# Score maxima from four 32x32 array tiles, score stacks kept per head in DRAM, and a lagged inverse DFT step

## The chip, the cores and the metric

The kernel runs on one core of one Trainium2 chip. The metric is the time of one execution on the device in microseconds (us); lower is better. Before the change three runs took 1411.7, 1414.9 and 1418.0 us, median 1414.9 us. A core has a matrix engine (TensorE, rows PE and PEld), a vector engine (VectorE, DVE), a scalar engine (ScalarE, ACT), GpSimd (POOL) and SyncE (SP), whose queue issues nearly all DMA transfers here. Each takes its instructions in order; they wait for each other through semaphores.

## The reference, cut to what matters

Two branches that share nothing are computed and put side by side in the output:

```python
def _A_ref(x, wqkv, wo):                      # x [1,2048,576], sliding-window attention
    B, S, D = x.shape
    H = 32; Dh = D // H; W = 256
    qkv = (x @ wqkv).reshape(B, S, 3, H, Dh).transpose(2, 0, 3, 1, 4)
    q, k, v = qkv[0], qkv[1], qkv[2]
    scores = einsum("bhqd,bhkd->bhqk", q, k) * (Dh ** -0.5)
    mask = (idx[:, None] - idx[None, :] >= 0) & (idx[:, None] - idx[None, :] < W)
    p = softmax(where(mask, scores, -1e9))
    o = einsum("bhqk,bhkd->bhqd", p, v)
    return o.transpose(0, 2, 1, 3).reshape(B, S, D) @ wo

def _B_ref(u, A, B, C, log_dt, Dskip):        # u [1,2048,576], S4 convolution
    K = real(sum_n C * dt*B * exp(dt*A*l))    # 2048 taps of each of 576 channels
    y = irfft(rfft(pad(u)) * rfft(pad(K)))[:2048]
    return y + u * Dskip

out = concatenate([_A_ref(...), _B_ref(...)], axis=-1)
```

32 heads of 18 channels; a query sees the 256 keys up to its own position.

## The kernel before

**Stage one (0 to 475 us)** interleaves three generators: `proj` (Q, K and V in f16 hi/lo pairs; Q and K written to DRAM as `qd`, V as `vd`), `tables` (the taps of the convolution) and `s1_u` (first DFT step of u, written to `gx`). `s1_k` does the same for the taps (`gk`). In `qd` there are three planes of 1152 rows: for a query row hi, lo, hi, for a key row hi, hi, lo. 54 rows, three planes of a head's 18 channels, stand under one another in a *stack*, so that one product gives hi·hi + lo·hi + hi·lo.

**The attention stage (from about 537 us)** is written out by hand: `attention` runs over 16 units, half `hf` of the queries by group `g` of four heads, and cuts a unit into six items (`c`, `bank`). For each item `merge` interleaves `scores` of the item (score matmuls L640 into PSUM `ST`, the exponential on ACT L642, masks on POOL L651), seven of the 32 steps of `gmax` of the *next* unit, `values` of the item two back (L663 into `po`), and two or three steps of `conv`. Python order is the order of each engine's queue. The sixth item of a unit has no `gmax` step left.

- `gmax` finds each query's maximum over its window. For 32 queries of four heads a block-diagonal tile `qh` (96 rows by 128 columns, loaded with the other heads' places zero) is the stationary operand: one matmul (L602) gives the scores of 128 rows by 288 keys, a second (L605, or L608 at the sequence's start) adds the mask from `bias`, and DVE takes the maximum (L610). The 128x32 maxima are turned (L614) and written by four small DMAs (L619) into row 54 of `Q`, against a key row of -32768: so the next unit's scores come out with the maximum subtracted. The PSUM pool `ring`, three banks, is shared by `gmax`, `conv` and the output projection.
- `load_unit(i + 1)` (eight stack loads L587 and L588, V by L591) and `load_gmax(i + 2)` (four loads into `qh` in pieces of 64 bytes, L575, one of `kh`, L577) are issued on SP at the start of unit i. Both exist in two sets.
- `norm` divides by the softmax's sum: `den` gathers the sum rows by a DMA (L678), reciprocal on DVE (L680), to DRAM `rd` (L682), back as `rb` on all 128 partitions (L684), the multiplication on DVE (L687), a hi/lo pair (L689, L690), and four DMAs to `od` (L693). It goes on by one `yield` per item.
- `conv` does 16 pairs of frequencies by two halves `hs`: four products (L477) with u's and the taps' first step, complex multiplication on DVE (t, L493 to L498; Y, L502 and L503), and the inverse (L507), whose result an ACT or DVE copy puts into `ho`, then DRAM `h`. After all pairs, 16 rounds `qd` read `h` back (L518) and u (L522), multiply u by the skip weight on POOL (L530), do the last inverse (L534), add on DVE (L536) and store (L539).
- `wo(0)` runs the output projection of the first half from item 62, `wo(1)` that of the second after everything else.

Of the kernel before, what the change touches and what calls it, by code (L numbers as in the profile page):

```python
# [97 lines left out]
def conv_steps(n):  # L98

    return (n + 1) * 225 // 96 - n * 225 // 96  # L100


class Kernel:
# [50 lines left out]

    def proj(self):
        nc, a, wp, dp, sp = self.nc, self.a, self.p["wq"], self.p["dram"], self.p["const"]
        self.qd = dp.tile([3, 1152, L], F16, name="qd")
# [33 lines left out]
        for c in range(4):  # L191
# [13 lines left out]
            for m in range(9):  # L205
                ps = self.p["pps"].tile([128, 512], F32, name="pp")
                self.mm14(ps, (wh, wl), (xh, xl), slice(m * 128, m * 128 + 128), slice(0, 512))
                st = self.p["pst"].tile([128, 2, 512], F16, name="qst")
                nc.scalar.activation(st[:, 0], ps, AF.Copy, scale=S)  # L209
                nc.vector.scalar_tensor_tensor(st[:, 1], ps, S, st[:, 0], op0=OP.mult, op1=OP.subtract)  # L210
                for r0, r1, two, one in ((0, D, slice(0, 2), 2), (D, 2 * D, slice(0, 3, 2), 1)):
                    r0, r1 = max(r0, m * 128), min(r1, m * 128 + 128)
                    if r0 < r1:
                        v = st[r0 - m * 128:r1 - m * 128]
                        nc.sync.dma_start(self.qd[two, r0:r1, cs].rearrange("a p c -> p a c"), v)
                        nc.sync.dma_start(self.qd[one, r0:r1, cs], v[:, 0])
                yield
# [239 lines left out]
    def conv(self):  # L457
# [22 lines left out]

        nx = load(0)
        for fp in range(16):
            cu, nx = nx, load(fp + 1) if fp < 15 else None
            ho = fs.tile([128, 2, D], F32, name="ho")
            for hs in range(2):
                X = fy.tile([128, 2, 288], F32, name="X")
                t1 = fy.tile([128, 2, 288], F32, name="t1")
                t2 = fy.tile([128, 2, 288], F32, name="t2")
                for p in range(2):
                    self.evac(X[:, p], s2(cu["w2"], cu["tx"], p, hs))  # L490
                    yield
                kr = s2(cu["w2"], cu["tk"], 0, hs)
                tt(t1[:, 0], X[:, 0], kr, op=OP.mult)  # L493
                tt(t2[:, 1], X[:, 1], kr, op=OP.mult)
                yield
                ki = s2(cu["w2"], cu["tk"], 1, hs)
                tt(t2[:, 0], X[:, 1], ki, op=OP.mult)
                tt(t1[:, 1], X[:, 0], ki, op=OP.mult)  # L498
                Y = [fy.tile([128, 288], F32, name="Y%d" % par) for par in range(2)]
                for par in range(2):  # L500
                    sl = slice(64 * par, 64 * par + 64)
                    tt(Y[par][0:64], t1[sl, 0], t2[sl, 0], op=OP.subtract)  # L502
                    tt(Y[par][64:128], t1[sl, 1], t2[sl, 1], op=OP.add)  # L503
                yield
                for par in range(2):
                    ps = ring()
                    nc.tensor.matmul(ps, cu["i1"][:, par, :], Y[par], start=True, stop=True)  # L507
                    self.evac(ho[:, par, hs * 288:hs * 288 + 288], ps)
                    yield
            nc.sync.dma_start(self.h.rearrange("a l f d -> (a l) f d")[:, 2 * fp:2 * fp + 2, :], ho)  # L510
# [3 lines left out]
        def loadh(qd):  # L514
            hp = fs.tile([128, 2, D], F32, name="ho")
# [4 lines left out]
            ut = fs.tile([128, D], F32, name="tx")  # L520
            for k in range(4):
                nc.sync.dma_start(ut[32 * k:32 * k + 32], uw[4 * qd + k])  # L522
# [19 lines left out]
    def att_setup(self):  # L542
# [10 lines left out]
        for b in range(2):  # L553
            d = {"q": ap.tile([96, 32, 4, 32], F16, name="qh%d" % b), "k": ap.tile([96, HK], F16, name="kh%d" % b),
                 "Q": ap.tile([128, 2, HQ], F16, name="Q%d" % b), "K": ap.tile([128, 2, HK], F16, name="K%d" % b)}
            nc.gpsimd.memset(d["q"], 0.0)
            nc.vector.memset(d["k"][64:96], 0.0)
# [12 lines left out]
    def load_gmax(self, i):  # L570

        nc, (hf, g), d = self.nc, divmod(i, 8), self.sets[i % 2]
        q0, k0, kc, kn = self.cols(hf)
        for j in range(4):
            nc.sync.dma_start(d["q"][18 * j:18 * j + 18, :, j, :],  # L575
                              self.qd[0, 72 * g + 18 * j:72 * g + 18 * j + 18, q0:q0 + HQ].rearrange("p (s q) -> p s q", q=32))
        nc.sync.dma_start(d["k"][0:72, kc:kc + kn], self.qd[0, D + 72 * g:D + 72 * g + 72, k0:k0 + kn])  # L577

    def load_unit(self, i):

        nc, (hf, g), d = self.nc, divmod(i, 8), self.sets[i % 2]
        q0, k0, kc, kn = self.cols(hf)
        t0, tn = k0 // 128, kn // 128
        for u in range(2):
            for b in range(2):
# [4 lines left out]
        nc.vector.memset(V[:, 760:], 0.0)  # L590
        nc.sync.dma_start(V[:, 760 - 76 * tn:760].rearrange("p (t e) -> p t e", e=76), self.vd[g][:, t0:t0 + tn])  # L591
        self.V[i] = V

    def gmax(self, i):
        nc, (hf, g), d = self.nc, divmod(i, 8), self.sets[i % 2]
        m = self.p["m"].tile([128, 32], F32, name="m")
        for t in range(32):
# [4 lines left out]
            nc.tensor.matmul(ps[:, :n], d["q"][:, t].rearrange("p j q -> p (j q)"), d["k"][:, k0:k0 + n],  # L602
                             start=True, stop=False, skip_group_check=True)
# [69 lines left out]
    def norm(self, i):  # L673
# [4 lines left out]
        nc.sync.dma_start(den, osb[18:128:32])  # L678
# [5 lines left out]
        nc.sync.dma_start(rb, rd.unsqueeze(1).to_broadcast([4, 32, HQ]))  # L684
# [4 lines left out]
        nc.scalar.activation(h[:, 0], osb, AF.Copy)  # L689
        nc.vector.tensor_tensor(h[:, 1], osb, h[:, 0], op=OP.subtract)  # L690
        for j in range(4):
            f0 = 72 * g + 18 * j
            nc.sync.dma_start(self.od[:, f0:f0 + 18, HQ * hf:HQ * hf + HQ].rearrange("a p n -> p a n"),  # L693
                              h[32 * j:32 * j + 18])
        yield

# [96 lines left out]
    def build(self):  # L793
        nc, a = self.nc, self.a
        with ExitStack() as es:
# [29 lines left out]
            with ExitStack() as e1:  # L825
# [5 lines left out]
                for n, b, s in (("fs", 2, None), ("fy", 2, None), ("att", 1, None), ("m", 2, None), ("P", 4, None),  # L831
                                ("v", 3, None), ("o", 2, None), ("n", 2, None), ("wo", 1, None), ("wo2", 2, None),
# [37 lines left out]
```

## Time and profile before

The profiled execution took 1412.87 us, its span 1411.2 us; the granted TensorE clock was 0.828 of full speed on average.

| engine | busy us | share of the span |
|---|---|---|
| PE, matmuls | 974.2 | 69% |
| PEld, weight loads | 473.1 | 34% |
| DVE | 713.4 | 51% |
| ACT | 610.4 | 43% |
| POOL | 338.6 | 24% |

167.06 MB went over the DMA queues, 161.30 MB of it issued by SP. Busy PE time holds matmuls from issue to modelled end, so that one which waits in the array counts as busy. A wait is named by who ended it. The attention stage is read by its units: the boundaries used here are the issue times of the V load (L591), which comes once in a unit.

### The profile page before, as it was taken

The page shows a single profiled execution, that of the slowest core. Times are in us where ns is not written, and L with a number is a line of the kernel's source. Part 1 is how long each engine was busy: PE and PEld are TensorE (multiplying, and loading weights), DVE is VectorE, ACT ScalarE, POOL GpSimd, SP SyncE. Part 2 cuts the span into 40 slices and gives each one's busy share as a digit, 9 for nine tenths or more (in the row PEclk, how much of TensorE's full clock was granted, in tenths as well). Part 3 has the DMA queues.
Part 4 walks back from the last instruction along what each step waited for, and adds up shares of the span by engine and source line. Part 5 has one row for each costly group of instructions (what it writes and reads, how often), then busy time and mean ns, then how long its engine had stood idle before and what let it go on. Part 6 is the DMA issues. An engine that isn't in the chain of part 4 may idle for free.

```text
span 1411.2 us, 25678 instructions
## 1 busy us (share of the span) xinstructions
PE 974.2 (69%) x10314; PEld 473.1 (34%) x10314; DVE 713.4 (51%) x1369; ACT 610.4 (43%) x907; POOL 338.6 (24%) x340
## 2 busy tenths in 40 slices
PE   1538898898889873777756686687678667645537
PEld 0224464464555431232212232233234333111115
DVE  3797667677662441555625565466445435322110
ACT  2767687687762311343423343344333324212212
POOL 0024344353440100222211122122112112323310
PEclk9759999999999985878857688899889889766769
DMA  9553143233224664234334424345335333556632
GB/s 240 156 175 115 59 114 87 81 83 103 70 55 135 185 181 124 68 118 112 115 85 114 133 63 136 110 126 144 87 105 150 76 120 87 137 153 168 170 94 101
DMA packets 199112, 167.06 MB, mean 118 GB/s; under 512 B 72945, under 2 KB 171057, under 8 KB 198801
## 3 DMA queue, kind: packets, MB, share of 16 engines
q1 hardware_dynamic: 197440, 161.30, 40.3%
q10 hardware_dynamic: 1504, 3.99, 1.1%
q8 instruction: 81, 1.33, 0.4%
q14 instruction: 39, 0.31, 0.1%
q0 software_dynamic: 48, 0.13, 0.0%
HBM read 103.11 MB, written 61.87 MB: 117 GB/s over the span
## 4 chain that ended last, share of the span: by engine, by line
PE 35%; DMA 21%; DVE 18%; SPq 12%; ACT 7%; issue 6%; POOL 1%; DVEq 0%; ACTq 0%; POOLq 0%
PE pp L153 7%; SPq L575 6%; PE po L663 4%; PE r L477 4%; PE r L153 4%; PE r L602 3%; DMA Q<-qd 3%; PE kp L395 3%; PE ST L640 3%; DMA rb<-rd 3%; PE pp L438 2%; PE r L507 2%; DMA den<-osb 2%; DVE m L610 2%; DMA oh<-od 2%
## 5 line engine op out<-in xcount | busy, mean ns | idle before, releaser
L642 ACT ACTIVATE P<-ST,esc 128x1024 f32<-128x1024 f32 (+1 forms) x192 | 202.9, 1060 | 291.9 <-PE ST L640 285.4
L651 POOL TENSOR_SCALAR_AFFINE_SELECT P<-P 128x512 f32<-128x512 f32 x240 | 156.3, 681 | 597.1 <-ACT P L642 597.0
L610 DVE TENSOR_REDUCE m<-r 128x1 f32<-128x288 f32 (+7 forms) x512 | 198.2, 430 | 167.5 <-PE r L605 117.6
L602 PE MATMUL r<-kh,qh 96*128 96x288 f16 (+7 forms) x512 | 144.2, 316 | 94.6 <-DVE m L610 59.3
L357 POOL TENSOR_TENSOR m<-A,tr 128x1024 f32<-128x1024 f32 x72 | 149.8, 2103 | 192.5 <-PE kp L395 145.8
L663 PE MATMUL po<-P,V 128*32 128x256 f32 (+2 forms) x1408 | 133.7, 458 | 4.5 <-ACT osb L671 2.1
L395 PE MATMUL kp<-Q,m 128*32 128x64 f32 x4608 | 87.0, 229 | 28.1 <-DVE Q L378 10.7
L640 PE MATMUL ST<-Q,K 64*128 64x384 f16 (+2 forms) x704 | 85.3, 313 | 22.3 <-DMA Q<-m 14.5
L602 PEld LDWEIGHTS <-qh 96*128 96x128 f16 x512 | 54.7, 108 | 115.9 <-issue 78.2
L395 PEld LDWEIGHTS kp<-Q,m 128*32 128x32 f32 x4608 | 74.3, 115 | 55.5 <-issue 41.1
L605 PE MATMUL r<-bias,idb 128*128 128x64 bf16 x448 | 91.2, 210 | 0.0
L507 PE MATMUL r<-Y,i 128*128 128x288 f32 x128 | 63.5, 587 | 35.6 <-DVE Y L503 13.2
L438 PE MATMUL pp<-ut,w 128*128 128x288 f32 x128 | 51.3, 525 | 45.0 <-DMA ut<-in_u_dram 27.5
L605 PEld LDWEIGHTS <-idb 128*128 128x128 bf16 x448 | 46.6, 104 | 91.8 <-issue 86.0
L534 PE MATMUL r<-ho,i 128*64 128x288 f32 x128 | 31.4, 580 | 62.7 <-DMA ho<-h 60.4
L477 PE MATMUL r<-tx,w 128*64 128x288 f32 x256 | 53.1, 499 | 30.2 <-DMA tx<-gx 22.5
L536 DVE TENSOR_TENSOR tk<-r,tx 128x288 f32<-128x288 f32 x32 | 14.3, 455 | 100.7 <-POOL tx L530 87.8
L153 PE MATMUL r<-woh,oh 128*128 128x288 f16 x160 | 29.5, 320 | 49.5 <-DMA oh<-od 49.4
L788 ACT ACTIVATE ya<-r,osc 128x288 f32<-128x288 f32 x32 | 16.0, 501 | 102.8 <-PE r L153 83.7
L210 DVE SCALAR_TENSOR_TENSOR qst<-pp,qst 128x512 f16<-128x512 f32 x36 | 24.7, 686 | 64.1 <-ACT qst L209 64.1
L153 PEld LDWEIGHTS <-oh 128*128 128x128 f16 x320 | 33.1, 107 | 68.1 <-DMA oh<-od 51.0
L116 ACT ACTIVATE g<-pp 128x288 f32<-128x288 f32 (+1 forms) x84 | 34.6, 447 | 45.7 <-DMA gk<-g 21.8
(150 smaller groups left out, 1667.2 us busy)
## 6 DMA issues: line engine op xcount, KB each, us to landing
gx<-g SPq DMA_DIRECT2D x32, 288.0 KB
gk<-g SPq DMA_DIRECT2D x16, 576.0 KB
tx<-gx SPq DMA_DIRECT2D x16, 576.0 KB
tk<-gk SPq DMA_DIRECT2D x16, 576.0 KB
h<-ho SPq DMA_DIRECT2D x16, 576.0 KB
ho<-h SPq DMA_DIRECT2D x64, 144.0 KB
raw<-in_xT_dram SPq DMA_DIRECT2D x16, 512.0 KB
qd<-qst SPq DMA_DIRECT2D x32, 256.0 KB
```

What stands on the lines that cost most here:

```text
L153: self.nc.tensor.matmul(ps, u, v, start=(i == 0), stop=(i == len(ops) - 1))
L357: self.nc.gpsimd.tensor_tensor(m, A[:, ch, a0:a0 + 8].unsqueeze(3).to_broadcast(sh), tr[:, ch, part, 0:8].unsqueeze(2).to_broadcast(sh), o ...
L395: nc.tensor.matmul(kp[32 * st:32 * st + 32, c % 2 * JJ2 + j, :], m[:, ch, a0:a0 + 32], Q[:, ch, term % 2, :], start=(term == 0), stop=(ter ...
L477: nc.tensor.matmul(ps[64 * par:64 * par + 64], w2[:, par, 64 * part:64 * part + 64], t[:, 2 * hs:2 * hs + 2, par, :], start=True, stop=True)
L507: nc.tensor.matmul(ps, cu["i1"][:, par, :], Y[par], start=True, stop=True)
L602: nc.tensor.matmul(ps[:, :n], d["q"][:, t].rearrange("p j q -> p (j q)"), d["k"][:, k0:k0 + n], start=True, stop=False, skip_group_check=True)
L605: nc.tensor.matmul(ps[:, :288].rearrange("p (a b) -> p a b", b=32)[:, 0:9:8], self.idb, self.bias, start=False, stop=True, skip_group_chec ...
L610: nc.vector.tensor_reduce(m[:, t:t + 1], ps[:, :n], axis=AX.X, op=OP.max)
L640: nc.tensor.matmul(ps[:, u, o:o + n], d["K"][h, jp, k0:k0 + 128], d["Q"][h, jp, q0:q0 + n], start=True, stop=True, skip_group_check=True)
L642: nc.scalar.activation(pt[:, 2 * jp:2 * jp + 2, lo:hi], ps[:, :, lo:hi], AF.Exp, scale=self.esc)
L651: nc.gpsimd.affine_select(v, v, pattern=[[0, 4], [sg, 128]], compare_op=OP.is_ge, fill=0.0, base=-1 if far else 0, channel_multiplier=-sg)
L663: nc.tensor.matmul(self.po[32 * j:32 * j + 32, t0 * 128:t1 * 128], V[:, kb * 76 + 19 * j:kb * 76 + 19 * j + 32], pt[:, j, o:o + (t1 - t0) ...
```

## The change

- `proj`: the Q and K columns of `wqkv` are put in another order on the host, channel by channel with the 64 heads of a channel side by side, so that a projection tile of 128 rows holds two channels of all heads. `store_heads` writes 54 rows of a head as one block of `qd`: hi, hi, lo for queries and hi, lo, hi for keys. Six DMAs per tile replace two (four in one tile).
- `gmax` uses the stacks `Q` and `K` of `scores`: their first 32 rows, which hold 18 hi·hi and 14 of the 18 cross products. Four matmuls per step, each on an array tile of 32 rows by 32 columns, replace the one. `qh`, `kh` and `load_gmax` go.
- Three sets of `Q` and `K` instead of two; `load_unit(i + 2)` at the start of unit i, four stack loads instead of eight. V loads, `od` stores and u loads are issued by POOL instead of SP.
- `norm`: `den` and `rb` in four DMAs each, one more item between `den` and its reciprocal and one between the hi and lo halves.
- `conv`: Y on POOL instead of DVE; the inverse of a half step is issued after the next half's Y; its copies and X's are all on ACT; the next pair is loaded in the middle of a pair; `h` rounds are loaded two ahead, after six empty steps. 232 steps are spread over the 96 items instead of 225.

```diff
 def conv_steps(n):
-    return (n + 1) * 225 // 96 - n * 225 // 96
+    return (n + 1) * 232 // 96 - n * 232 // 96
...
+    def store_heads(self, st, i, cs):
+        nc = self.nc
+        stack = lambda o, n: self.qd[18 * o:18 * o + 54 * n, cs].rearrange("(h a r) c -> h a r c", a=3, r=18)[:, :, i]
+        nc.sync.dma_start(stack(1, 64)[:, 0:2], st)
+        nc.sync.dma_start(stack(0, 32)[:, 0], st[0:32, 0])
+        nc.sync.dma_start(stack(97, 32)[:, 2], st[32:64, 0])
...
-                        nc.sync.dma_start(self.qd[two, r0:r1, cs].rearrange("a p c -> p a c"), v)
-                        nc.sync.dma_start(self.qd[one, r0:r1, cs], v[:, 0])
+                for e in range(2):
+                    self.store_heads(st[64 * e:64 * e + 64], 2 * m + e, cs)
...
+        def inverse(fp, hs, i1, Y, ho):
+            for par in range(2):
+                ps = ring()
+                nc.tensor.matmul(ps, i1[:, par, :], Y[par], start=True, stop=True)
+                nc.scalar.activation(ho[:, par, hs * 288:hs * 288 + 288], ps, AF.Copy)
+                yield
+            if hs == 1:
+                nc.sync.dma_start(self.h.rearrange("a l f d -> (a l) f d")[:, 2 * fp:2 * fp + 2, :], ho)
...
-                    tt(Y[par][0:64], t1[sl, 0], t2[sl, 0], op=OP.subtract)
-                    tt(Y[par][64:128], t1[sl, 1], t2[sl, 1], op=OP.add)
+                    nc.gpsimd.tensor_tensor(Y[par][0:64], t1[sl, 0], t2[sl, 0], op=OP.subtract)
+                    nc.gpsimd.tensor_tensor(Y[par][64:128], t1[sl, 1], t2[sl, 1], op=OP.add)
                 yield
+                if last:
+                    yield from inverse(*last)
+                last = fp, hs, cu["i1"], Y, ho
+                if hs == 0 and fp < 15:
+                    nx = load(fp + 1)
...
-                nc.sync.dma_start(ut[32 * k:32 * k + 32], uw[4 * qd + k])
+                nc.gpsimd.dma_start(ut[32 * k:32 * k + 32], uw[4 * qd + k])
...
-        nx = loadh(0)
-        yield
+        nx = [loadh(0), loadh(1)]
+        for _ in range(6):
+            yield
...
         for u in range(2):
-            for b in range(2):
-                r = 72 * g + 36 * b + 18 * u
-                nc.sync.dma_start(d["Q"][64 * u:64 * u + 54, b], self.qd[:, r:r + 18, q0:q0 + HQ])
-                nc.sync.dma_start(d["K"][64 * u:64 * u + 54, b, kc:kc + kn], self.qd[:, D + r:D + r + 18, k0:k0 + kn])
+            nc.sync.dma_start(d["Q"][64 * u:64 * u + 54], heads(216 * g, q0, HQ)[u])
+            nc.sync.dma_start(d["K"][64 * u:64 * u + 54, :, kc:kc + kn], heads(32 * 54 + 18 + 216 * g, k0, kn)[u])
...
-            nc.tensor.matmul(ps[:, :n], d["q"][:, t].rearrange("p j q -> p (j q)"), d["k"][:, k0:k0 + n],
-                             start=True, stop=False, skip_group_check=True)
+            for j in range(4):
+                r = slice(64 * (j % 2), 64 * (j % 2) + 32)
+                nc.tensor.matmul(ps[32 * j:32 * j + 32, :n], d["Q"][r, j // 2, 32 * t:32 * t + 32],
+                                 d["K"][r, j // 2, k0:k0 + n], start=True, stop=False, skip_group_check=True)
...
-        nc.sync.dma_start(den, osb[18:128:32])
+        for j in range(4):
+            nc.sync.dma_start(den[32 * j:32 * j + 32], osb[32 * j + 18:32 * j + 19])
+        yield
         yield
...
-        nc.sync.dma_start(rb, rd.unsqueeze(1).to_broadcast([4, 32, HQ]))
+        for j in range(4):
+            nc.sync.dma_start(rb[32 * j:32 * j + 32], rd[j].partition_broadcast(32))
...
-                    self.load_unit(i + 1)
                     if i < 14:
-                        self.load_gmax(i + 2)
+                        self.load_unit(i + 2)
...
-                                ("v", 3, None), ("o", 2, None), ("n", 2, None), ("wo", 1, None), ("wo2", 2, None),
+                                ("v", 4, None), ("o", 3, None), ("n", 2, None), ("wo", 1, None), ("wo2", 2, None),
```

The order of instructions on PE, in the second unit (i = 1), at one `gmax` step behind `values` (`po`) and an inverse of `conv` (`r<-Y`). Before:

```order
L663 MATMUL po<-P,V 32x128 x4
L507 MATMUL r<-Y_6555,i_6161 128x288
L602 LDWEIGHTS qh_5942
L602 MATMUL r<-kh_5943,qh_5942 128x288
L605 LDWEIGHTS idb
L605 MATMUL r<-bias,idb 128x2x32
```

After the change, at such a place:

```order
L670 MATMUL po<-P,V 32x256 x4
L488 MATMUL r<-Y_6798,i_6533 128x288
L609 LDWEIGHTS Q_6092
L609 MATMUL r<-K_6093,Q_6092 32x288
L609 LDWEIGHTS Q_6092
L609 MATMUL r<-K_6093,Q_6092 32x288
L609 LDWEIGHTS Q_6092
L609 MATMUL r<-K_6093,Q_6092 32x288
L609 LDWEIGHTS Q_6092
L609 MATMUL r<-K_6093,Q_6092 32x288
L612 LDWEIGHTS idb
L612 MATMUL r<-bias,idb 128x2x32
```

One pair of weight load and matmul on the whole array has become four pairs on tiles of 32x32, and the mask's matmul on the whole array still follows each group of four.

SP at the start of a unit, from the stack loads to the softmax sum of the unit before. Before:

```order
L587 DMA Q_5955<-qd 54x1x1024
L588 DMA K_5956<-qd 54x1x1024
L591 DMA V<-vd 128x608
L575 DMA qh_5942<-qd 18x32x32 x4
L577 DMA kh_5943<-qd 72x1024
L678 DMA den<-osb 128x1x32
L682 DMA rd<-den 128x32
L684 DMA rb<-rd 128x1x1024
```

After:

```order
L591 DMA Q_6078<-qd 54x2x1024
L592 DMA K_6079<-qd 54x2x1024
L591 DMA Q_6078<-qd 54x2x1024
L592 DMA K_6079<-qd 54x2x1024
L492 DMA h<-ho 128x1152
L469 DMA w_6905<-in_c_w_dram 128x256
L469 DMA i_6907<-in_c_i_dram 128x256
L472 DMA tx<-gx 128x4x288
L472 DMA tk<-gk 128x4x288
L686 DMA den<-osb 32x1x32 x4
L691 DMA rd<-den 128x32
L694 DMA rb<-rd 32x1024 x4
```

The five `gmax` loads and V are gone from ahead of `den`, and the loads of `conv` stand in their place.

POOL within a unit, after the change (before, it held nothing but L651 rows there, 136 in a row):

```order
L595 DMA V<-vd 128x608
L516 TENSOR_TENSOR Y_7793<-t_7709,t_7710 64x288
L517 TENSOR_TENSOR Y_7793<-t_7709,t_7710 64x288
L516 TENSOR_TENSOR Y_7794<-t_7709,t_7710 64x288
L517 TENSOR_TENSOR Y_7794<-t_7709,t_7710 64x288
L658 AFFINE_SELECT P<-P 128x4x128 x2
L704 DMA od<-oh_7762 18x2x1024 x4
L658 AFFINE_SELECT P<-P 128x4x128
L516 TENSOR_TENSOR Y_8003<-t_7894,t_7895 64x288
```

Y and three kinds of DMA have come in between the masks (L658), which wait for nobody but ACT's exponential.

More of the change, by code (lines that the diff above doesn't have):

```diff
@@ L210, in proj @@
                 nc.vector.scalar_tensor_tensor(st[:, 1], ps, S, st[:, 0], op0=OP.mult, op1=OP.subtract)
[L211 to L216, printed above, removed]
+                for e in range(2):
+                    self.store_heads(st[64 * e:64 * e + 64], 2 * m + e, cs)
                 yield
@@ L479, in s2 @@
             return ps
+        def inverse(fp, hs, i1, Y, ho):
[6 more added lines that the diff above has]
+                nc.sync.dma_start(self.h.rearrange("a l f d -> (a l) f d")[:, 2 * fp:2 * fp + 2, :], ho)
         nx = load(0)
+        last = None
         for fp in range(16):
-            cu, nx = nx, load(fp + 1) if fp < 15 else None
+            cu = nx
             ho = fs.tile([128, 2, D], F32, name="ho")
@@ L501, in conv @@
                     sl = slice(64 * par, 64 * par + 64)
-                    tt(Y[par][0:64], t1[sl, 0], t2[sl, 0], op=OP.subtract)
-                    tt(Y[par][64:128], t1[sl, 1], t2[sl, 1], op=OP.add)
+                    nc.gpsimd.tensor_tensor(Y[par][0:64], t1[sl, 0], t2[sl, 0], op=OP.subtract)
+                    nc.gpsimd.tensor_tensor(Y[par][64:128], t1[sl, 1], t2[sl, 1], op=OP.add)
                 yield
[L505 to L508, printed above, removed]
-                    yield
-            nc.sync.dma_start(self.h.rearrange("a l f d -> (a l) f d")[:, 2 * fp:2 * fp + 2, :], ho)
+                if last:
[3 more added lines that the diff above has]
+                    nx = load(fp + 1)
+        yield from inverse(*last)
         outv = a["out"][:, D:2 * D].rearrange("(p l) d -> l p d", l=64)
@@ L514, in loadh @@
         def loadh(qd):
-            hp = fs.tile([128, 2, D], F32, name="ho")
+            hp = fs.tile([128, 2, D], F32, name=("ho", "tx")[qd % 2])
             for l in range(2):
@@ L519, in loadh @@
                                       self.h[part, 4 * qd + l:4 * qd + 4:2].rearrange("k f d -> f k d"))
-            ut = fs.tile([128, D], F32, name="tx")
+            ut = fy.tile([128, D], F32, name=("X", "t1")[qd % 2])
             for k in range(4):
-                nc.sync.dma_start(ut[32 * k:32 * k + 32], uw[4 * qd + k])
+                nc.gpsimd.dma_start(ut[32 * k:32 * k + 32], uw[4 * qd + k])
             return hp, ut
-        nx = loadh(0)
-        yield
+        nx = [loadh(0), loadh(1)]
+        for _ in range(6):
+            yield
         for qd in range(16):
-            (hp, ut), nx = nx, loadh(qd + 1) if qd < 15 else None
-            y = fs.tile([128, D], F32, name="tk")
+            if qd < 14:
+                nx.append(loadh(qd + 2))
+            hp, ut = nx[qd]
+            y = fy.tile([128, D], F32, name="t2")
             nc.gpsimd.tensor_tensor(ut, ut, self.dsk, op=OP.mult)
@@ L552, in att_setup @@
         self.sets = []
-        for b in range(2):
[L554 to L557, printed above, removed]
+        for b in range(3):
+            d = {"Q": ap.tile([128, 2, HQ], F16, name="Q%d" % b), "K": ap.tile([128, 2, HK], F16, name="K%d" % b)}
             nc.vector.memset(d["Q"], 0.0)
@@ L626, in scores @@
     def scores(self, i, c, bank):
-        nc, d, bb = self.nc, self.sets[i % 2], self.blocks(i, c, bank)
+        nc, d, bb = self.nc, self.sets[i % 3], self.blocks(i, c, bank)
         pt = self.p["P"].tile([128, 4, 512], F32, name="P")
@@ L689, in norm @@
         nc.scalar.activation(h[:, 0], osb, AF.Copy)
+        yield
         nc.vector.tensor_tensor(h[:, 1], osb, h[:, 0], op=OP.subtract)
```

30 lines of the change are left out of this document (11 added, 19 removed).

## The prediction

> **What bounds the kernel now.** First the page's chain by line, then the busy time of the engines in stretches that end where a unit's V load is issued: unit 0, units 1 to 3, 4 to 6, 7 to 9, 10 to 13, 14 and 15, and the end.
>
> ```profile
> PE pp L153 7%; SPq L575 6%; PE po L663 4%; PE r L477 4%; PE r L153 4%; PE r L602 3%; DMA Q<-qd 3%; PE kp L395 3%; PE ST L640 3%; DMA rb<-rd 3%; PE pp L438 2%; PE r L507 2%; DMA den<-osb 2%; DVE m L610 2%; DMA oh<-od 2%
> ```
>
> ```profile
> 537.00:598.00 61.00, 35.89 (x241) 13.37 (x242) 23.79 (x64) 17.20 (x23) 9.76 (x16) 0.68 0.35 104
> 598.00:723.00 125.00, 94.72 (x692) 36.17 (x692) 69.74 (x171) 49.03 (x65) 27.36 (x42) 0.81 0.37 107
> 723.00:886.00 163.00, 108.27 (x741) 40.87 (x743) 84.58 (x202) 54.80 (x75) 26.96 (x44) 0.73 0.39 112
> 886.00:1008.00 122.00, 87.80 (x710) 33.62 (x710) 70.68 (x164) 51.62 (x64) 30.07 (x46) 0.87 0.41 115
> 1008.00:1232.00 224.00, 158.35 (x1248) 72.52 (x1247) 100.03 (x231) 75.84 (x101) 46.78 (x67) 0.84 0.40 114
> 1232.00:1349.00 117.00, 60.65 (x451) 18.48 (x447) 27.06 (x61) 28.34 (x29) 37.80 (x43) 0.69 0.61 160
> 1349.00:1411.00 62.00, 31.26 (x224) 22.50 (x224) 2.80 (x3) 9.48 (x18) 0.00 (x0) 0.81 0.28 93
> ```
>
> After the stretch's length come the busy times of PE, PEld, DVE, ACT and POOL, then the granted clock. No engine is full: at best (886 to 1008) PE is busy 72% and DVE 58%, and a unit takes 41 us; units 4 to 6 take 54, units 10 to 13 56, the last two 58. So the attention stage is bound by waits, and the clock is lowest where they are longest (0.73, 0.69). The chain names the queue of SP: L575, the loads of `qh`, is its second entry. One unit shows how; SP's rows, then the chain in the order of time:
>
> ```profile
> 927.36 11.60 SPq L575 DMA_DIRECT2D qh<-qd  x4
> ...
> 939.71 0.61 SPq L678 DMA_DIRECT2D den<-osb  x1
> ```
>
> ```profile
> 939.71 2.65 DMA den<-osb
> ...
> 956.79 3.58 DMA Q<-m
> ...
> 989.28 4.28 DMA rb<-rd
> ```
>
> Four loads hold SP for 11.60 us, and only then is the softmax sum fetched. DVE, which takes its work in order, stands at the reciprocal until it lands, and everything that DVE has to take out of `ring` stands behind it. PE works on through part of this, so the chain's 6% is no promise: what it costs has to be read from waits. These are the long ones between 537 and 1349 us (total, times, longest):
>
> ```profile
> DVE den L680 <- DMA den<-osb: 36.2, 7, 10.4
> DVE amxo L143 <- DMA raw<-in_wo_dram: 19.9, 2, 11.9
> DVE osb L687 <- DMA rb<-rd: 12.3, 3, 5.7
> ACT woh L762 <- DMA raw<-in_wo_dram: 11.8, 1, 11.8
> PE r L153 <- DMA oh<-od: 22.4, 2, 14.2
> PE r L477 <- DMA tx<-gx: 22.5, 1, 22.5
> PE r L534 <- DMA ho<-h: 60.4, 12, 14.1
> DVE tk L536 <- POOL tx L530: 87.8, 14, 16.8
> ```
>
> **Waits that go.** The normalisation gets an item (about 41/6 = 7 us) more ahead of the reciprocal, and `den` no longer stands behind L575: the 36.2 and the 12.3 us go, and I take 50. The Q<-m wait (3.58 us in the unit shown) stays, since the maxima still have to land before the next scores. Of the other transfers held up on SP, the output weights' 19.9 + 11.8 = 31.7 us should nearly all go (25), half of the 22.4 for `oh`, which is still asked for at the moment of use (11), and of the first `tx` the part that SP spent on `qh`, some 10 of 22.5. Together 96 us of units 0 to 13.
>
> **What takes their place on PE and DVE.** PE's rows in a stretch at full clock:
>
> ```profile
> 983.03 0.19 PE L605 MATMUL r<-bias,idb 128*128 128x64 bf16 x1
> 983.07 0.29 PE L602 MATMUL r<-kh,qh 96*128 96x288 f16 x1
> 983.19 0.19 PE L605 MATMUL r<-bias,idb 128*128 128x64 bf16 x1
> 983.32 0.39 PE L640 MATMUL ST<-Q,K 64*128 64x128 f16 x4
> 983.64 0.64 PE L663 MATMUL po<-P,V 128*32 128x256 f32 x8
> 984.21 0.71 PE L477 MATMUL r<-tk,w 128*64 128x288 f32 x4
> ```
>
> The first number is the start. From the mask's matmul to the next score matmul, both on the whole array, pass 0.04 us; to L640, on tiles of 64x128, 0.13. A change of tile shape thus costs about 0.1 us. The eight matmuls of L663 (four column tiles, twice) fill 0.57 us up to the next start, less 0.1 for that change 0.24 us per four, while the group's mean for one is 458 ns (first row of the next fence): four column tiles run side by side. One L602 streams in 983.19 - 983.07 = 0.12 us. If the four 32x32 matmuls also run side by side, a `gmax` step keeps its 0.12 and pays for shape changes: into 32x32, and out to the mask. In the order of instructions I count 794 changes of shape in the attention stage before and 1616 after; 822 x 0.1 = 82 us at full clock, 5.1 per unit. Against it, DVE is relieved:
>
> ```profile
> L663 PE MATMUL po<-P,V 128*32 128x256 f32 (+2 forms) x1408 | 133.7, 458 | 4.5 <-ACT osb L671 2.1 <-POOL P L651 1.5 <-issue 0.6
> L610 DVE TENSOR_REDUCE m<-r 128x1 f32<-128x288 f32 (+7 forms) x512 | 198.2, 430 | 167.5 <-PE r L605 117.6 <-PE r L608 47.3
> L651 POOL TENSOR_SCALAR_AFFINE_SELECT P<-P 128x512 f32<-128x512 f32 x240 | 156.3, 681 | 597.1 <-ACT P L642 597.0
> L502 DVE TENSOR_TENSOR Y<-t,t 64x288 f32<-64x288 f32 x64 | 31.2, 487 | 0.7
> L530 POOL TENSOR_TENSOR tx<-tx,dsk 128x576 f32<-128x576 f32 x16 | 22.5, 1404 | 86.7 <-DMA tx<-in_u_dram 83.3 <-DVE m L610 3.4
> L118 DVE COPY ho<-r 128x288 f32<-128x288 f32 x32 | 14.6, 455 | 30.8 <-PE r L507 30.6
> ```
>
> L502 is half of Y; the two halves are 62 us, the copies of `ho` 14.6: 77 us, 4.8 per unit, against 198.2 us of maxima that stay. The copies move to ACT, which is busy 42% at best. PE and DVE feed each other through three `ring` banks, so the two nearly cancel; I put the net at 0. The ends are +5.1 x 14 = +71 us (all on PE's path) and -4.8 x 14 = -67 (PE's changes fall into its waits). With fewer waits the clock should go from 0.81 towards the 0.87 of the best units: 7% of the 449 us that PE is busy between 598 and 1232, half of it on the path, 15 us.
>
> On POOL, Y is 128 instructions of 288 columns. L530's rate gives 1404 x 288/576 = 0.70 us each, 5.6 per unit; on DVE they took 0.49, and I keep 0.49 to 1.4 (no gain for half the columns) as ends. Masks are 156.3/16 = 9.8 per unit. The only DMA that POOL issues in this trace took it 0.86 us:
>
> ```profile
> L801 POOL DMA_DIRECT2D w<-in_c_w_dram x1: 862/862/862, 1.3 to 1.3; - x1
> ```
>
> Five per unit (V, four `od`) make 4.3 us; ends 0.3, as SP's rows below, and 1.7, twice that row. POOL then has 20 us of work in a unit of 35: it is covered, since Y is wanted only after the next half step and masks two items later.
>
> **The last two units.** One round of `conv`'s second part on SP:
>
> ```profile
> 1244.98 1.76 SPq L522 DMA_DIRECT2D tx<-in_u_dram  x4
> 1246.84 1.77 SPq L539 DMA_DIRECT2D out_dram<-tk  x4
> 1248.71 1.78 SPq L518 DMA_DIRECT2D ho<-h  x4
> ```
>
> 5.3 us, 85 for 16 rounds in a stretch of 117; u moves to POOL, which leaves 57. Loads run two rounds ahead instead of one, which is aimed at the 60.4 us of PE and the 87.8 us of DVE above. I take 30 off the 117; the ends are 0 (POOL, busy 37.8 there, gets 64 x 0.86 = 55 us more) and 50.
>
> **The two ends of the program.** In the tail, after unit 15, only the normalisation and the projection are left; in stage one SP's stores of `qst` are the question:
>
> ```profile
> 1353.24 8.12 DMA rb<-rd
> ```
>
> ```profile
> 222.03 0.33 SPq L216 DMA_DIRECT2D qd<-qst  x1
> 222.76 0.36 SPq L215 DMA_DIRECT2D qd<-qst  x1
> ```
>
> `rb` in four parts should land like the other transfers of the normalisation (2.65 and 4.28 above): 5 us less. The ends are 0 and 7. The Trainium skill bears on this row: by "DMA: Bandwidth & Descriptors", section "Why a DMA increments its semaphore by 16 and not by 1", a DMA spreads over the largest number up to 16 that divides the slowest dimension of both sides. That would be 4 engines for `rb` before (512 KB) and 16 now, and with that page's 27 GiB/s per engine an estimate of 4.5 us against 1.1; by it the tail would gain 3.4, not 5. No run here shows it so far. In stage one 216 stores replace 80: 136 x 0.35 = 48 us of SP. There are 36 projection tiles in some 370 us, ten us each, and six stores take 2.1 of them; I add 5, ends 0 and 48.
>
> **Sum.** The profiled execution took 1412.9 us, 2 below the median and inside the runs' 1411.7 to 1418.0. 1412.9 - 96 - 15 + 0 - 30 - 5 + 5 = 1272.
>
> **Rivals.**
> *The four tiles run one after the other.* They write to one PSUM bank; the score matmuls L640, the only row tiles in this trace, write to two. Then a step takes 4 x 0.12, 0.36 us more, 512 x 0.36 = 184 us at full clock, on the engine that is busiest already: 1272 + 184 = 1456, slower than before. It decides from 141/512 = 0.28 us more per step. For it: no row shows tiles of different rows in one bank. Against it: L663's four write to one bank and overlap, as their rows show. The Trainium skill has a rule for it: "TensorEngine Tiling (Array Packing)", section "Restrictions and Gotchas", says that different row tiles cannot access the same PSUM bank simultaneously, and leaves the synchronization to software. By that rule this rival holds; no run here shows it so far.
> *POOL becomes what the others wait for.* With Y at 1.4 us and DMAs at 1.7, a unit has 9.8 + 11.2 + 8.5 = 30 us of POOL work in one order, and masks stand behind `od` stores that wait for DVE. Values and inverses come late by some 5 us per unit: 16 x 5 = 80, 1352.
> *PE's shape changes hide.* The units then follow DVE: 1272 - 67 = 1205. For it: in the best units 28% of PE's time is idle.
>
> **How the numbers follow.** Forecast 0.55, hidden changes 0.20, POOL 0.15, serial tiles 0.10. The range runs from 1195, a little under the hidden changes, to 1355, just over POOL; stage one's bound of 43 more fits in it. Left out are the serial tiles and some of the tails. Within 0.5% (7 us), about what a measurement of this kernel can tell from no change, lies almost nothing: 0.02. Faster 0.88; slower, the serial tiles, 0.10.
>
> **What would show it.** Units 1 to 9 near 36 us each; `den` and `rb` gone from DVE's waits; the starts of the four 32x32 matmuls a few ns apart (side by side) or 0.12 us (one by one); a mask's matmul 0.1 us behind their columns; POOL under 60% busy in the units; the last two units near 87 us; stage one within 5 us. The forecast is wrong if PE's busy share nears 95% in the units, if DVE or PE wait for Y or for masks, or if stage one grows by tens of us.

## The result, and the profile after

The changed kernel took **1307.5 us** (median of 4 runs, 1291.2 to 1323.7) where the kernel before took 1416.5 beside it: 0.919 of the time, interval 0.909 to 0.929. (Times are medians of all runs, but the ratio and its interval leave out the slowest run of after, 1323.7 us, so they are not 1307.5 over 1416.5.) In a second session, together with experiments, it took 1313.8 (1304.6 to 1321.9), 0.932 of before (0.927 to 0.937). So it is faster, and inside the predicted range, but 35 us above the predicted 1272.

The rows "of after" below are from the profiled execution of the second session (1314.65 us, span 1312.8). First the page's busy times, and the start of its chain by line:

```profile
PE 1064.8 (81%) x11850; PEld 493.6 (38%) x11850; DVE 659.6 (50%) x1196; ACT 624.6 (48%) x939; POOL 513.4 (39%) x626
...
PE r L609 9%; PE po L670 8%; PE pp L153 7%; PE r L481 7%; PE r L153 5%; PE ST L647 4%; PE r L612 4%; PE r L488 4%; DMA gk<-g 3%; PE kp L399 2%; PE pp L442 2%; DMA Q<-m 1%; PE x L295 1%; DMA K<-in_wqkv_dram 1%; DVE tr L339 1%
```

SP's queue, `den` and `rb` have gone from the chain's first lines; PE rows now fill it, the new 32x32 matmuls (L609) and the mask (L612) in front. The stretches say what that means. Columns as in the prediction: units 0 to 13, units 14 and 15, and the tail, of before and then of after. The boundaries are others than in the prediction, because after the change V is loaded two units ahead: here a stretch begins with the first exponential (`P<-ST`) of unit 0 or of unit 14, and the tail with the end of the last `osb` copy. In before, unit 14 so begins at 1219 us, 13 before the 1232 of the prediction.

```profile
533.00:1219.00 686.00, 479.18 (x3590) 194.72 (x3592) 345.60 (x820) 247.91 (x326) 136.68 (x209) 0.80 0.39 111
1219.00:1349.00 130.00, 66.50 (x487) 20.30 (x483) 30.27 (x68) 29.82 (x31) 42.06 (x49) 0.70 0.60 157
1349.00:1411.00 62.00, 31.26 (x224) 22.50 (x224) 2.80 (x3) 9.48 (x18) 0.00 (x0) 0.81 0.28 93
```

```profile
535.00:1168.00 633.00, 565.62 (x4958) 216.01 (x4958) 282.57 (x650) 261.36 (x357) 291.69 (x439) 0.77 0.40 117
1168.00:1252.00 84.00, 66.10 (x558) 20.34 (x554) 31.79 (x65) 30.95 (x32) 63.93 (x94) 0.74 0.71 192
1252.00:1313.00 61.00, 31.68 (x224) 22.78 (x224) 2.80 (x3) 9.06 (x17) 4.60 (x8) 0.78 0.30 97
```

Stage one ends where it did (533 and 535), the tail is as long as it was, the last two units lost 46 us and the other fourteen 53. In those, PE is now busy 565.62 of 633 us, 89% against 70%, and its granted clock went down from 0.80 to 0.77, not up. Four stretches of after show how the clock goes:

```profile
808.90:863.50 54.60, 48.49 (x510) 19.60 (x506) 31.76 (x73) 28.18 (x40) 31.75 (x46) 1.00 0.41 125
863.50:907.90 44.40, 42.41 (x294) 13.22 (x294) 15.96 (x36) 14.53 (x19) 16.33 (x27) 0.50 0.30 89
918.10:965.90 47.80, 47.45 (x323) 14.71 (x323) 18.21 (x42) 16.78 (x22) 17.49 (x28) 0.50 0.29 81
1003.50:1058.10 54.60, 50.16 (x515) 23.80 (x512) 24.19 (x56) 25.19 (x35) 24.78 (x38) 1.00 0.35 108
```

The clock is either whole or half. At half, 323 matmuls fill 47.80 us to 99%; at full clock, 510 take 54.60. By the trace's records of the clock, 350 of the 732 us from 520 us to the last `osb` copy are at half (before: 362 of 829).

Two steps of `gmax` at full clock, then one at half, show what a step costs PE (start, length):

```profile
620.83 0.30 PE L609 MATMUL r<-K,Q 32*32 32x288 f16 x4
621.07 0.20 PE L612 MATMUL r<-bias,idb 128*128 128x64 bf16 x1
621.20 0.30 PE L609 MATMUL r<-K,Q 32*32 32x288 f16 x4
...
921.92 0.42 PE L609 MATMUL r<-K,Q 32*32 32x288 f16 x4
922.27 0.23 PE L612 MATMUL r<-bias,idb 128*128 128x64 bf16 x1
922.44 0.42 PE L609 MATMUL r<-K,Q 32*32 32x288 f16 x4
```

Four matmuls together last 0.30 us; one of them lasts 0.292 (median), and within a group the starts in the trace are 3 ns apart. **They run side by side.** From their start to the mask's pass 0.24 us at full clock: 0.12 for the 288 columns, and 0.1 for the change of tile shape. At half clock 0.36 pass (median of 191 steps, counted from the first of the four), where the kernel before, without a shape change there, needs 0.215 from the columns' start to the mask's: the shape change costs 0.14 us. So at full clock a step costs PE 0.37 us where the matmul and the mask before took 0.12 + 0.04, by the starts in the prediction's rows of L602 and L605.

The waits of units 0 to 13 that the prediction spoke of, in after:

```profile
PE r L153 <- DMA oh<-od: 15.2, 2, 8.1
...
PE r L609 <- DVE m L617: 12.1, 10, 5.2
...
PE r L481 <- DMA tx<-gx: 10.3, 1, 10.3
...
DVE amxo L143 <- DMA raw<-in_wo_dram: 3.1, 2, 2.6
DVE osb L697 <- DMA rb<-rd: 2.8, 4, 1.5
```

DVE's 36.2 us for `den` are gone altogether, of 12.3 for `rb` 2.8 are left, of `raw` 3.1. The forecast of which waits would go was right. That the units got only 53 us shorter is the question.

### The profile page after: what moved, and what is told of

Same layout as the page of the kernel before. It is cut to its first block, busy times and chain, and to the rows that moved or that the text cites. A ratio compares the mean times of both kernels' runs of the same rounds, so it can differ in the third digit from the quotient of the medians.

```text
span 1321.8 us, 28952 instructions
## 1 busy us (share of the span) xinstructions
PE 1077.9 (82%) x11850; PEld 494.3 (37%) x11850; DVE 660.5 (50%) x1196; ACT 624.8 (47%) x939; POOL 515.2 (39%) x626
## 4 chain that ended last, share of the span: by engine, by line
PE 57%; DMA 13%; DVE 12%; ACT 7%; issue 4%; POOL 4%; SPq 3%; DVEq 0%; ACTq 0%; POOLq 0%
PE r L609 10%; PE po L670 8%; PE r L481 7%; PE pp L153 7%; PE r L153 5%; PE ST L647 5%; PE r L612 4%; PE r L488 4%; DMA gk<-g 3%; PE kp L399 3%; PE pp L442 2%; PE x L295 1%; DMA K<-in_wqkv_dram 1%; DMA Q<-m 1%; DVE tr L339 1%
## 5 line engine op out<-in xcount | busy, mean ns | idle before, releaser
L617 DVE TENSOR_REDUCE m<-r 128x1 f32<-128x288 f32 (+7 forms) x512 | 212.1, 435 | 261.8 <-PE r L612 213.9
L658 POOL TENSOR_SCALAR_AFFINE_SELECT P<-P 128x512 f32<-128x512 f32 x240 | 151.1, 659 | 254.8 <-ACT P L649 252.5
L609 PE MATMUL r<-K,Q 32*32 32x288 f16 (+8 forms) x2048 | 180.7, 343 | 24.1 <-DVE m L617 15.0
L670 PE MATMUL po<-P,V 128*32 128x256 f32 (+2 forms) x1408 | 145.0, 493 | 8.7 <-POOL P L658 5.9
L609 PEld LDWEIGHTS <-Q 32*32 32x32 f16 x2048 | 53.6, 92 | 170.6 <-issue 149.1
L516 POOL TENSOR_TENSOR Y<-t,t 64x288 f32<-64x288 f32 x64 | 52.2, 816 | 146.0 <-DVE t L511 144.1
L647 PE MATMUL ST<-Q,K 64*128 64x384 f16 (+2 forms) x704 | 90.2, 330 | 16.3 <-DMA Q<-m 16.1
L612 PE MATMUL r<-bias,idb 128*128 128x64 bf16 x448 | 97.6, 218 | 0.0
L442 PE MATMUL pp<-ut,w 128*128 128x288 f32 x128 | 51.4, 527 | 42.6 <-DMA ut<-in_u_dram 25.2
L612 PEld LDWEIGHTS <-idb 128*128 128x128 bf16 x448 | 44.3, 99 | 86.5 <-issue 57.0
L481 PE MATMUL r<-tx,w 128*64 128x288 f32 x256 | 57.7, 539 | 10.1 <-DMA tx<-gx 10.1
L517 POOL TENSOR_TENSOR Y<-t,t 64x288 f32<-64x288 f32 x64 | 58.2, 909 | 3.7
L481 PE MATMUL r<-tk,w 128*64 128x288 f32 x256 | 58.5, 545 | 1.1 <-DVE t L508 1.0
```

The costliest lines, as they stand in the source:

```text
L481: nc.tensor.matmul(ps[64 * par:64 * par + 64], w2[:, par, 64 * part:64 * part + 64], t[:, 2 * hs:2 * hs + 2, par, :], start=True, stop=True)
L609: nc.tensor.matmul(ps[32 * j:32 * j + 32, :n], d["Q"][r, j // 2, 32 * t:32 * t + 32], d["K"][r, j // 2, k0:k0 + n], start=True, stop=False ...
L612: nc.tensor.matmul(ps[:, :288].rearrange("p (a b) -> p a b", b=32)[:, 0:9:8], self.idb, self.bias, start=False, stop=True, skip_group_chec ...
L617: nc.vector.tensor_reduce(m[:, t:t + 1], ps[:, :n], axis=AX.X, op=OP.max)
L647: nc.tensor.matmul(ps[:, u, o:o + n], d["K"][h, jp, k0:k0 + 128], d["Q"][h, jp, q0:q0 + n], start=True, stop=True, skip_group_check=True)
L658: nc.gpsimd.affine_select(v, v, pattern=[[0, 4], [sg, 128]], compare_op=OP.is_ge, fill=0.0, base=-1 if far else 0, channel_multiplier=-sg)
```

## The experiments

My theory: PE now bounds the units, by what a step of small tiles costs it, in shape changes (the cost) and in a lower clock. For the clock two readings stood against each other: it is granted by how much of the array the matmuls fill (array share), or by how long PE is busy (time share). The rival to the cost: the units are still set by waits, on SP, POOL or DVE, and a cheaper step changes nothing. All ratios are to the kernel before, run on the same chip (medians 1409.6 to 1410.0). Three kernels first changed the small tiles, and one added work.

**The mask by four matmuls on the same 32x32 tiles** (no shape change between columns and mask):

```
-nc.tensor.matmul(ps[:, :288]..., self.idb, self.bias, ...)
+for j in range(4):
+    nc.tensor.matmul(o[:, :288]..., self.idb[r:r + 32, r:r + 32], self.bias[r:r + 32], ...)
```

> The changed kernel with the mask of a maxima step added by four matmuls on the same 32x32 tiles instead of one on the whole array, so that no shape change is left inside a step. Cost theory (shape changes are what the tiles cost): 512 changes into the mask and most of those back to the tiles go, some 700 x 0.1 = 70 us at full clock and more at half; the time falls from 1307 to 1220-1245. Wait theory (PE's changes hide in its waits): within 15 us of the changed kernel.

1256.6 us, 0.889 (0.885 to 0.893): 51 below the 1307.5 (42 to 60 us by the ratios, against 0.919 and 0.932). Of 1610 changes of tile shape in the attention stage's matmuls 867 are left, and a step at full clock, from one start of L609 to the next, takes 0.16 us, as before the change, and not 0.37:

```profile
654.58 0.30 PE L609 MATMUL r<-K,Q 32*32 32x288 f16 x4
654.72 0.20 PE L614 MATMUL r<-bias,idb 32*32 32x64 bf16 x4
654.74 0.29 PE L609 MATMUL r<-K,Q 32*32 32x288 f16 x4
```

743 changes fewer at 0.1 us are 74 us; 51 of them arrived, so the step's cost does bear on the units, though the expected 1220 to 1245 was missed by 12.

**54 rows in place of 32**, and **both together**, with the mask on 64x32 tiles:

```
-r = slice(64 * (j % 2), 64 * (j % 2) + 32)
+r = slice(64 * (j % 2), 64 * (j % 2) + 54)
...
-    nc.tensor.matmul(o[:, :288]..., self.idb[r:r + 32, r:r + 32], self.bias[r:r + 32], ...)
+    nc.tensor.matmul(o[:, :288]..., self.idb[r:r + 64, r:r + 32], self.bias[r:r + 64], ...)
```

> The changed kernel with 54 rows of the stacks in the maxima's matmuls instead of 32: same columns, same number of instructions, but array tiles of 64x32. Array-share theory (the clock is granted by the share of the array's cells that is at work; the 32x32 tiles put a quarter of the array to work and keep it at half clock): the half-clock time in the attention stage falls from 417 us to under 300 and the time by 30 to 80 us. Time-share theory (only the time in which columns stream counts): clock and time as the changed kernel, 1291 to 1324.

> Both edits: 54 rows, and the mask by four matmuls on the same 64x32 tiles. If shape changes and array share both count, the fastest of all, 1170-1220. If only the shape changes count, the same as the kernel with the mask on 32x32 tiles alone.

1284.7, 0.912 (0.907 to 0.917), and 1233.7, 0.874 (0.871 to 0.877). The same number of matmuls, columns and shape changes, only with more rows of the array in use, brings the time at half clock from 350 to 283 us and the whole 9 to 27 us down (0.912 against 0.919 and 0.932; the first of these lies within the intervals, the second does not). The times at half clock are counted from 520 us to the last `osb` copy; the 417 us of the expectation are those of the slowest run of after, counted to its end. A clearer pair is the two kernels with the small mask, run side by side: there more rows bring the time at half clock from 256 to 164 us and the whole from 1256.6 to 1233.7, with intervals apart. Cheaper shape changes are not the reason: a step takes as long with 54 rows as with 32 at the same clock (0.37 us at full, 0.53 and 0.52 at half). So the rows in use do bear on the clock; by time share nothing would have changed. The size was forecast too large both times. The two edits add up: 51 and 23 below the 1307.5 each, 74 together.

**One more matmul on the whole array per step**, whose result the next overwrites:

```
+nc.tensor.matmul(ps[:, :n], self.idb, self.fill[:, :n], start=True, stop=True, ...)
```

> The changed kernel with one matmul more in each maxima step, on the whole array, 288 columns of ones whose result is overwritten by the step's own matmuls: 512 x 0.12 = 61 us more PE work at full clock. Array-share theory: the clock stays full for most of the attention stage (mean granted clock above 0.9 there), which gives back more than it costs: 1210-1280. Wait theory or plain PE bound: slower than the changed kernel by 50 to 100 us, 1350-1410.

1351.9, 0.960 (0.955 to 0.965). In units 0 to 13 the clock rose to 0.84, and the time at half clock, counted as above, fell from 350 to 266 us, yet units 0 to 13 take 666 us and not 633: here work put in for the clock's sake costs more than it returns.

Then the change was undone piece by piece. **The changed kernel again**, as the measure on that chip:

> The changed kernel itself, beside the three that undo one part of it each: every theory expects what it gave before, 0.91 to 0.93 of the kernel before.

1313.8, 0.932, at the upper edge. **The maxima from one matmul on the whole array**, with the loads that it needs, everything else as changed:

```
+d = {"q": ap.tile([96, 32, 4, 32], F16, name="qh%d" % b), "k": ap.tile([96, HK], F16, name="kh%d" % b)}
...
-for j in range(4):
-    r = slice(64 * (j % 2), 64 * (j % 2) + 32)
-    nc.tensor.matmul(ps[32 * j:32 * j + 32, :n], d["Q"][r, j // 2, 32 * t:32 * t + 32],
-                     d["K"][r, j // 2, k0:k0 + n], start=True, stop=False, skip_group_check=True)
+e = self.gsets[i % 2]
+nc.tensor.matmul(ps[:, :n], e["q"][:, t].rearrange("p j q -> p (j q)"), e["k"][:, k0:k0 + n],
+                 start=True, stop=False, skip_group_check=True)
...
+self.load_unit(i + 1)
...
-self.load_unit(i + 2)
+self.load_gmax(i + 2)
```

> The changed kernel with the maxima again from one matmul on the whole array (two sets of Q and K instead of three, and eight more loads per unit on SP). If the small tiles cost PE time and clock (822 shape changes of 0.1 us, and array share low enough that the clock stays at half), and the gain comes from the order of the loads and the normalisation: 1215 to 1265. If the gain comes from taking the loads of qh off SP, which this brings back: 1320 to 1400. In the first case the time at half clock in the units falls below 280 us.

1240.4, 0.879 (0.876 to 0.882): **73 us less**, as the cost has it and not the queue of SP, with 187 us at half clock. Its units 0 to 13:

```profile
530.00:1092.00 562.00, 441.11 (x3602) 184.48 (x3603) 274.54 (x647) 260.44 (x357) 293.06 (x441) 0.88 0.50 140
```

The eight loads per unit that are back on SP hold it for 126 us in all, nearly as long as the five of before (147 us), but not all waits came back with them: of DVE's waits for `den` only one of 4.7 us did, of those for `rb` 10.3 us.

**The normalisation as before** (no extra items, one DMA each for `den` and `rb`), and, in the next session, **u, V and `od` back on SP**:

```
-for j in range(4): nc.sync.dma_start(den[32 * j:32 * j + 32], osb[32 * j + 18:32 * j + 19])
-yield
+nc.sync.dma_start(den, osb[18:128:32])
...
-nc.gpsimd.dma_start(ut[32 * k:32 * k + 32], uw[4 * qd + k])
+nc.sync.dma_start(ut[32 * k:32 * k + 32], uw[4 * qd + k])
```

> The changed kernel with the normalisation as before (reciprocal an item earlier, den and rb one DMA each). By the prediction's term the waits for den and rb return: 40 to 60 us more than the changed kernel, of which 5 are in the tail. If the queue of SP alone made them long, den now lands in some 3 us and all of it costs under 15 us more.

> The changed kernel with the DMAs that went to POOL (u, V and the od stores) back on SP. If SP is no longer what anything waits for once qh is gone: within 15 us of the changed kernel. If the last two units were held by SP's issue time (28 us of u there) and od stores block the maxima's transfers: 25 to 60 us more, most of it after unit 13.

1337.0, 0.947 (0.943 to 0.950), and 1331.2, 0.942 (0.938 to 0.947): 23 and 17 us more, each between its two expectations. Where they lose is plain from the stretches; first the normalisation's, then SP's:

```profile
537.00:1162.00 625.00, 552.77 (x4927) 213.06 (x4928) 278.25 (x644) 261.11 (x357) 278.27 (x423) 0.78 0.39 116
1162.00:1263.00 101.00, 71.24 (x585) 21.95 (x584) 31.23 (x69) 30.39 (x31) 73.52 (x113) 0.71 0.67 179
1263.00:1329.00 66.00, 34.78 (x224) 24.05 (x224) 2.80 (x3) 9.08 (x17) 2.35 (x4) 0.71 0.25 85
```

```profile
538.00:1163.00 625.00, 563.86 (x4967) 215.55 (x4971) 283.63 (x651) 262.72 (x357) 245.48 (x353) 0.77 0.41 118
1163.00:1261.00 98.00, 70.35 (x549) 20.60 (x545) 29.80 (x63) 30.38 (x31) 38.18 (x45) 0.67 0.66 172
```

In units 0 to 13 neither costs anything (625 us against 633); they lose 17 and 14 us in the last two units, and the old normalisation 5 in the tail. These are the shortest of four executions each, 7 us below their medians, and where the 7 went isn't seen.

**The first part of `conv` as before**, and **only Y back on DVE**:

```
-nc.gpsimd.tensor_tensor(Y[par][0:64], t1[sl, 0], t2[sl, 0], op=OP.subtract)
+tt(Y[par][0:64], t1[sl, 0], t2[sl, 0], op=OP.subtract)
```

> The changed kernel with the first part of conv as before (Y on DVE, the inverse step not lagged, evacuations spread as before). If DVE's relief was worth what the prediction set against PE's shape changes (4.8 us per unit): 40 to 70 us more. If PE alone sets the units: within 15 us.

> The changed kernel with only Y back on DVE (the lag, the later prefetch and the evacuations on ACT stay). If DVE's 62 us for Y are what the whole first part was worth: 50 to 83 us more than the changed kernel. If the lag of the inverse step was worth it: under 25 more.

1397.0, 0.988 (0.980 to 0.995), and 1377.9, 0.977 (0.968 to 0.986): 83 and 64 us more. PE's share of busy time had made me doubt that relief for DVE was worth anything. It is worth about what was moved, 64 us by the medians (48 to 76 for the four runs, 1362 to 1390 us) for the 62 us of Y: with Y on DVE, PE's wait for the reader of the maxima goes from 12.1 to 26.9 us, and the clock of units 0 to 13 from 0.77 to 0.74, in the shortest run:

```profile
535.00:1218.00 683.00, 585.90 (x4963) 221.80 (x4963) 342.75 (x779) 263.79 (x357) 187.08 (x311) 0.74 0.37 109
```

The other 19 us, of the lag, the later prefetch and the evacuations, are no larger than that spread and were not taken apart.

**Both undone**, the whole-array maxima and the first part of `conv`. What is left of the change is what acts on waits and on the end.

> Both undone: the maxima from one matmul on the whole array, and the first part of conv as before. If the two terms are separate (73 us of PE's tiles, 83 us of conv): 1310 to 1335. If conv's change is worth something only while the small tiles fill PE: 1235 to 1270. If each hides the other: above 1340.

1310.4, 0.929 (0.925 to 0.932): the two terms are separate (1240.4 + 70), and undoing both gives the changed kernel's time again to 3 us.

**The fastest version:** 54 rows and the mask on 64x32 tiles, with `oh` and `ol` for both chunks of a half loaded together, those of the first half from item 56 on.

```
+lds = [load(2 * hf), load(2 * hf + 1)]
+yield
...
+if n == 56:
+    next(wo0)
```

> The version with 54 rows and the mask on 64x32 tiles (0.874 of before, 1233.7), with oh and ol of the first two chunks loaded some items ahead. PE waited 42 us there for oh, five times: if that wait is on the path, 15 to 35 us less, 1200 to 1220; if PE's other work would have come late anyway, under 8 us less.

**1216.1** (1215.9 to 1216.7), 0.863 of before (0.860 to 0.865), 0.93 of the changed kernel: 17.6 us less than without the early loads, at the lower end of what was expected. Its five waits of PE for `oh` (42.6 us) became one of 22.4, in the tail, where the last unit's `od` has to be waited for.

## Why the prediction was right, and where it was 35 us off

**The two terms set to a net of 0 were right, and so were their ends.** For PE's shape changes the end was +71; the whole-array kernel shows 73. For DVE's relief it was -67; undone it costs 83 beside small tiles and 70 without them. That 73 meets 71 so closely is in part luck: the 71 were shape changes alone, and of the 73 the mask on small tiles gave back 51 and more rows of the array, through the clock, another 23. Together the runs give between +3 (1313.8 less the 1310.4 with both undone) and -10. What I had not seen is that both work through the clock too: without the small tiles PE is busy 441 us in units 0 to 13, with them 566, and part of the difference is the same columns at half clock.

**The step that failed is "Together 96 us of units 0 to 13", with the 15 us of clock on top.** The kernel with both net terms undone isolates it. It ran 634 us in units 0 to 13, where before took 686: 52, not 111. Its stretch and waits, with the one row of before that the prediction did not show ahead of them:

```profile
PE r L602 <- DVE m L610: 58.3, 32, 10.4
```

```profile
529.00:1163.00 634.00, 478.38 (x3610) 194.52 (x3610) 351.59 (x811) 250.14 (x325) 189.52 (x313) 0.82 0.45 124
```

```profile
PE r L623 <- DVE m L631: 31.3, 23, 4.1
...
PE r L153 <- DMA oh<-od: 24.5, 3, 12.8
...
PE r L481 <- DMA tx<-gx: 14.4, 1, 14.4
...
DVE den L703 <- DMA den<-osb: 3.8, 1, 3.8
```

The waits of DVE and ACT did go: `den` from 36.2 to 3.8, `raw` from 31.7 to 6.5, and all that DVE waited for DMAs from 72 to 10 us. But the price is paid on PE. Its busy time is the same (479 and 478 us); what went is its idle time, 207 us before and 156 here, 51 less. Added up by who ended them, PE's waits for DVE went from 101 to 87 us, for ACT from 32 to 14, for DMAs from 60 to 51; 10 us in which PE waited for nothing that the profile shows went too. So DVE waited 62 us less for DMAs, but PE only 15 us less for DVE. PE's own three long rows, for the reader of the maxima, for `oh` and for `tx`, were 58.3 + 22.4 + 22.5 = 103 us before and are 31.3 + 24.5 + 14.4 = 70 here: 33 us less. I had written that PE works on through part of DVE's wait and that its cost has to be read from waits, and then booked the waits of DVE and ACT one for one, 75 us of `den`, `rb` and `raw`. PE's rows of the same view were the place to read the gain from, and its longest, 58.3 us, was not in my list. The clock rose by 0.02 here, not by the 0.06 that made 15 us. Of the single waits, `tx` (10 forecast) gave 8 here and 12 in after, `oh` (11) gave 7 in after and nothing here.

Units 1 to 9 took 43.5 us each in after (45.6 before), counted from first exponential to first exponential, and not the 36 named as a sign; without the small tiles they take 36.6.

The extra items of the normalisation, moreover, did nothing in those units; with the `qh` loads gone from SP, the old normalisation is as good there. The whole-array kernel has the `gmax` loads back and the spacing kept, and hardly waits for `den` either. So for `den` either cure was enough by these runs; for `rb` 10.3 of the 12.3 us came back with the loads. Both undone at once was not run.

**The last two units** were forecast 30 us shorter and are 46; they stand at 84 us, near the 87 named as a sign. Undone one at a time, moving u, V and `od` to POOL was worth 14 of it and the normalisation 17; the other 15, the loads two rounds ahead among them, were not undone. POOL's 0.86 us for a DMA was 0.51 for u, 0.59 for V and 0.60 for `od`; an instruction of Y, for which 0.70 us were taken, took it 0.86. POOL was busy 46% in units 0 to 13, and that rival fell: PE waits there for a mask 4.8 us in all, and for Y not at all.

**The ends of the program**: stage one +5 forecast, 0 and +2 measured (533 and 535 us against 533). In the tail, 5 us less were forecast and less than one came. The chain in the order of time, first of before (its `rb`, 8.12 us from 1353.24, stands in the prediction), then of after:

```profile
1349.43 1.96 DMA den<-osb
1351.79 1.43 DMA rd<-den
...
1366.12 2.39 DMA od<-oh
```

```profile
1253.33 2.21 DMA den<-osb
1256.05 1.43 DMA rd<-den
1258.83 2.86 DMA rb<-rd
...
1267.63 2.33 DMA od<-oh
```

Of a transfer in four parts the chain shows the last part. The first part of `rb` goes out at 1257.54, as soon as `rd` has landed, and the last lands at 1261.69: 4.15 us for the four in place of 8.12, 4.0 less where 5 were forecast. That agrees in direction with the rule cited from the Trainium skill, "DMA: Bandwidth & Descriptors", section "Why a DMA increments its semaphore by 16 and not by 1" (more engines for it), whose figures gave an estimate of 3.4. But the links around it grew. `den`, now four DMAs, takes from 1251.51, just behind the last `osb` copy, to 1255.54: 4.0 us in place of 2.0. From the landing of `rb` to the last `od`, which POOL issues now, pass 5.9 us in place of 4.8. From the `osb` copy to that `od` it is 16.1 us, 16.7 before. A DMA split into four pays in its issues: the last part leaves 1.8 us behind the first for `den` and 1.3 for `rb`.

With the sizes measured the sum reads 1412.9 - 52 (waits and clock) - 1 (net of the two terms, 633 against 634) - 46 - 1 + 2 = 1315, and the profiled execution took 1314.7. So 59 us too much were forecast for waits and clock and 16 too little for the last two units; the ends of the program nearly cancelled. With the boundary of before at the prediction's 1232 us the same times read as 65 and 33 in place of 52 and 46, that is 46 too much and 3 the other way; the sum and the step that failed stay the same. The range held, but not for the reason for which it was drawn: its upper end came from the rival of POOL, which fell, and its width took in a term of waits twice too large.

**Serial tiles** (1456) are out: 3 ns between starts, 0.30 us for four. The rule cited from the Trainium skill, "TensorEngine Tiling (Array Packing)", section "Restrictions and Gotchas", that different row tiles cannot access one PSUM bank at the same time, did not make these four wait for each other: the measured 3 ns decide. The four write to different quarters of the bank's 128 partitions; tiles that write the same partitions were not run. **Hidden shape changes** (1205) are out as well: taking 743 of them away gave 51 us.

Two things stay open. Why the clock goes to half is not shown: more rows in use kept it up, and so did extra columns, but no run set a threshold. And the 19 us between Y alone and the whole first part of `conv`, and 15 of the 46 us of the last two units, are not split.

## What to carry to other kernels

A wait of an engine off the critical path is not a gain to be booked one for one: here DVE waited 62 us less for DMAs, and PE 15 us less for DVE. Look up what the engine that fills the chain waits for, and price the term from its rows. When work is split over small array tiles, count the changes of tile shape (0.10 to 0.14 us each) and give neighbouring matmuls the same shape, here the mask: that took back most of the price, and more rows and earlier loads made the fastest kernel, 0.863 of before. Moving 62 us of DVE work off the hand-over between DVE and PE was worth about as much (48 to 76 us in four runs), although DVE was busy only half the time.

## What the runs showed of the hardware

A change of tile shape costs 0.10 us at full and 0.14 at half clock: the median from the first 32x32 start to the mask's is 234 ns over 257 steps at full and 358 ns over 191 at half, against 132 and 215 where the mask runs on the same tiles. Over a whole step, with two changes, it is 367 against 162 ns at full and 520 against 293 at half clock: 0.10 and 0.11 us a change. PE busy 99% of a stretch is no sign of a full clock: of the four stretches above the two at half clock are its busiest. And filling more rows of the array with the same instructions lowered the time at half clock from 350 to 283 us, and from 256 to 164 where the mask too ran on small tiles. Four matmuls on tiles of 32x32 in two groups of rows ran side by side although they write to one PSUM bank, each to its own quarter of the partitions.
